# q's second addend by an accumulating DMA, pairs of exponential tiles added on VectorE, the overflow chain in pieces, three splits earlier

## The chip, the cores and the metric

The kernel runs on one core of one Trainium2 chip. Its metric is the device time in microseconds (us) of the slowest core, here the only one; the time of a kernel is the median of its runs. Besides the timed runs there is one profiled execution, from which all rows below come.

## What is computed

Three stages follow each other, each on the result of the one before. The reference, cut to what matters:

```python
q_pool = q.reshape(B, H, S // 2, 2, D).mean(axis=3)       # B 2, H 8, S 1152, D 64
scores = scale * np.matmul(q_pool, k.transpose(0, 1, 3, 2))
attn = np.exp(scores - np.max(scores, axis=-1, keepdims=True))
attn = attn / (np.sum(attn, axis=-1, keepdims=True) + 1e-09)
x = np.matmul(attn, v)                                    # then (1152, 512)

e_idx = np.argmax(x @ w_gate, axis=1)                     # 8 experts, one for each token
...
h = np.maximum(x[mask] @ w1[e], 0.0)                      # 512 to 1024
out[mask] = gate_w[mask, None] * eom[mask, e, None] * (h @ w2[e])

h = x @ w_in                                              # 512 to 2048
g = h * np.tanh(log1p(exp(h)))
return g @ w_out                                          # 2048 to 512
```

The weights of the last stage come as 64-bit floats; the kernel makes 32-bit ones of them ("decodes" them) on VectorE.

## The kernel before, in words

The order of instructions on each engine is the order in which the program writes them; nothing reorders them, and an engine that waits holds all that is behind it in its own queue. Products in full precision are made of three products of a high and a low part (mm3): the high part is a copy to a rounded 32-bit type on ScalarE (act, L91), the low part the difference, on VectorE (tt, L94, or stt, L97).

**Attention** (0 to 300 us) works on eight pairs of heads. The loop over g (from L499) makes nine steps for each pair p, one for each tile t of 128 keys. A step writes, in the order of seq ("0mmrpsmMt", L520): the scores of tile t (scores, L240) with their exponentials on ScalarE into the tile Pt, "pt", which has four buffers; two chunks of row maxima of the next pair (max_chunk, L201: a matmul into one of three PSUM tiles "mx" and a maximum on VectorE, L103); for the step before, the products of exponentials and v (pv, L262) and the row sums of the exponentials (psums, L268: eight matmuls of 160 columns by e2); and one or two more chunks of maxima. Each chunk first takes one task of the step off a list (mxc). The tasks stand in a table (at_step, L411): the loading of the next pair's k and q (load_head, L159, on SP's queue), the sum of the two addends of q's mean (qsum, L174; VectorE, for two heads of 16 GpSimd), the high and low parts of q and k (qhi, qlo, khi, klo), the reciprocals of the pair before (sum_rec), its output (x_out, x_put). At the end of the tasks of the steps in DEC_T (L171) stands one piece of decoding (decode_step, L484): three pieces make a chunk, half of one of 16 tiles wd, and the pieces are one, two and two VectorE operations. The last pair has no maxima to make for a next one; each of its steps has three pieces. DEC_A is the number of chunks that attention decodes, DEC_M the number done when the experts end.

**Routing** (300 to 318 us) takes each token's expert and place. The experts (318 to 471 us) are eight slots of fixed room, three wide ones and five narrow ones; tokens without room go to an overflow loop (L1091 on), whose passes are left out where there are none. The slots' steps form one list, flat, and the loop over q (L1052) writes for step q the preparations of step q + 2 and then its products. The first layer makes hps and its high and low parts hh and hl; the second layer uses them with the parts w2h and w2l of w2. At q = 2 stands routing_over (L701): 28 operations on VectorE that find the overflowing tokens' places, from cap to oi. At q = 4 routing_oix (L742) takes oi through nine small matmuls (L745); then the routing's pool is closed and a pool mq is opened in its room, and from there pieces of decoding follow each step of a wide slot (DECS, L1017). One chunk of 32 is left for the last stage.

**The last stage** (477 to 701 us) makes 48 steps of zmm (first layer) and omm (second layer). Ahead of it the split of wd[0..2] into high and low parts (split_hi on ScalarE, split_lo on VectorE, L1119 to L1129), then ysplit (high and low parts yh, yl of three tiles of the stage's input, from PSUM), then the first zmm (L1162), which takes the PSUM banks that the tiles of ysplit leave.

Of the kernel before, what the change touches and what calls it, by code (L numbers as in the profile page):

```python
# [9 lines left out]
F32 = mybir.dt.float32  # L10
# [74 lines left out]
def kernel(ctx, tc, cst, qt, kt, v, wgo, w1, w2, wio, out):  # L85
# [295 lines left out]
    mq = []  # L381
    wraw, dmt, dst_ = {}, {}, {}

    def load_raw(i, pool):
        f, c = divmod(i, 2)
        wraw[i] = pool.tile([P, 512, 2], I32, name="wraw", bufs=2 if pool is ap else WRB if mq and pool is mq[0] else 1)
        (A if mq and pool is mq[0] else SP).dma_start(out=wraw[i].rearrange("p a b -> p (a b)"), in_=wio[f, :, 512 * c:512 * (c + 1)].bitcast(I32))

    def decode(i, part, pool):
        f, c = divmod(i, 2)  # L390
        lo, hi = wraw[i][:, :, 0], wraw[i][:, :, 1]
        dst = wd[f][:, 512 * c:512 * (c + 1)]
        if part == 0:
            m = dmt[i] = pool.tile([P, 512], F32, name="dm", bufs=2 if pool is ap or mq and pool is mq[0] else 1)
# [24 lines left out]
    for p in range(NPAIR):  # L419
        for h, (a, b) in enumerate((((p - 2, 4), (p - 1, 0)), ((p - 1, 0), (p - 1, 3)))):  # L420
# [3 lines left out]
            at_step(lp, lt, lambda p=p, h=h: load_head(p, h))  # L424
# [18 lines left out]
    load_head(0, 0)  # L443
# [15 lines left out]
    load_head(0, 1)  # L459
# [39 lines left out]
    for g in range(-9, 9 * NPAIR):  # L499
# [4 lines left out]
        tasks = list(sched.get(g, ()))  # L504
        if p == NPAIR - 1:
# [195 lines left out]
    def routing_over():  # L701
# [29 lines left out]
        red(od, ob, ALU.add)  # L731

# [7 lines left out]
        return oi  # L740
# [81 lines left out]
    def evac(s, j):  # L822
        y = yv[0] if s > E else mq[0].tile([P, DM], F32, name="y", bufs=3)
# [186 lines left out]

    HB = 3
# [5 lines left out]
    DECS = [[0, 0, 0, 0, 0, 2, 2, 2, 2, 2], [0, 2, 2, 2, 2, 2, 2, 2, 2, 0], [0, 2, 2, 2, 2, 2, 2, 2, 2, 2]]  # L1017
# [34 lines left out]
    for q, (n_, i, _, main, w_, _) in enumerate(flat):  # L1052
# [66 lines left out]
    def split_hi(b_, f):  # L1119
        if b_ == 0:  # L1120
            hi = zp.tile([P, 1024], F32R, name="wh", bufs=NF)
            ws2[f] = [hi]
            act(hi, wd[f])

    def split_lo(b_, f, eng=V):
        if b_ == 0:
            lo = cp.tile([P, 1024], F32R, name="wd", bufs=16) if f else zp.tile([P, 1024], F32R, name="wl0")
            tt(eng, lo, wd[f], ws2[f][0].bitcast(F32), ALU.subtract)
            ws2[f].append(lo)  # L1129
# [132 lines left out]
    for i in range(len(steps) + LAG):  # L1262
        if dec[0] < 32:
            for _ in range(3 if i == 1 else 0):
                decode_step(zy, 32)
            raw_ahead(zy, 32)
# [55 lines left out]
```

## Time and profile before

| | |
|---|---|
| median of 3 runs | 708.56 us (707.39 to 708.73) |
| the profiled execution | 703.0 us, of which the span of its instructions 701.2 us |
| mean granted clock of TensorE | 0.988 of full speed |
| busy share of the span | TensorE 94%, VectorE 71%, ScalarE 53%, GpSimd 18% |
| chain of work that ended last | TensorE 21%, VectorE 7%, issue 3%, ScalarE 1% |

The busy share is an average over the three stages. PE is TensorE's matmul unit, PEld its loading of weights, DVE VectorE, ACT ScalarE, POOL GpSimd, SP the engine that mostly issues DMAs. The profiled execution lies 5.6 us below the median.

### The profile page before, as it was taken

The page shows a single profiled execution, that of the slowest core. Times are in us where ns is not written, and L with a number is a line of the kernel's source. Part 1 is how long each engine was busy: PE and PEld are TensorE (multiplying, and loading weights), DVE is VectorE, ACT ScalarE, POOL GpSimd, SP SyncE. Part 2 cuts the span into 40 slices and gives each one's busy share as a digit, 9 for nine tenths or more (in the row PEclk, how much of TensorE's full clock was granted, in tenths as well). Part 3 has the DMA queues.
Part 4 walks back from the last instruction along what each step waited for, and adds up shares of the span by engine and source line. Part 5 has one row for each costly group of instructions (what it writes and reads, how often), then busy time and mean ns, then how long its engine had stood idle before and what let it go on. Part 6 is the DMA issues. An engine that isn't in the chain of part 4 may idle for free. (4 is left out here: it accounts for less than half of the span.)

```text
span 701.2 us, 12210 instructions
## 1 busy us (share of the span) xinstructions
PE 658.6 (94%) x4719; PEld 511.8 (73%) x4719; DVE 501.1 (71%) x1022; ACT 372.2 (53%) x752; POOL 127.2 (18%) x127
## 2 busy tenths in 40 slices
PE   5999999999999999949799999986899999999997
PEld 3766666666666666628696977656787899999995
DVE  6776868686868675455764856915999977897775
ACT  6656565656475636414345536434665554555543
POOL 5200000000000000024121423211322332233322
PEclk9999999999999999989999999998999999999999
DMA  6743332433332304139579869762000020001001
GB/s 226 266 144 132 114 117 98 133 114 132 115 124 76 97 18 122 38 107 338 194 251 391 308 247 357 273 251 70 0 1 1 1 91 1 0 1 46 2 0 45
DMA packets 24915, 88.37 MB, mean 126 GB/s; under 512 B 2694, under 2 KB 7439, under 8 KB 20754
## 3 DMA queue, kind: packets, MB, share of 16 engines
q1 hardware_dynamic: 20544, 74.15, 30.1%
q10 hardware_dynamic: 2466, 8.13, 3.3%
q0 software_dynamic: 1840, 5.25, 2.2%
q8 instruction: 38, 0.62, 0.4%
q14 instruction: 27, 0.22, 0.1%
HBM read 79.65 MB, written 8.39 MB: 126 GB/s over the span
## 5 line engine op out<-in xcount | busy, mean ns | idle before, releaser
L103 DVE TENSOR_REDUCE Mp<-mx 128x1 f32<-128x384 f32 x198 | 103.6, 551 | 62.1 <-PE mx L207 61.3
L91 ACT ACTIVATE pt<-sc 128x320 f32<-128x320 f32 (+1 forms) x216 | 97.2, 489 | 89.0 <-PE sc L251 85.5
L100 POOL TENSOR_SCALAR u<-u 128x384 f32<-128x384 f32 x48 | 60.2, 1254 | 155.9 <-ACT u L91 124.1
L266 PE MATMUL pv<-pt,vt 128*64 128x288 f32 x576 | 85.8, 418 | 1.0 <-DVE sm L94 0.5
L799 PE MATMUL zps<-yh,wh 128*128 128x384 f32 x188 | 64.2, 341 | 1.7 <-DVE n L97 1.7
L207 PE MATMUL mx<-at,qs 128*128 128x384 f32 x176 | 55.8, 380 | 8.3 <-DVE qs L97 7.9
L801 PE MATMUL zps<-yl,wh 128*128 128x384 f32 x188 | 63.5, 338 | 0.0
L800 PE MATMUL zps<-yh,wd 128*128 128x384 f32 x180 | 61.0, 339 | 0.0
L1224 PE MATMUL ops<-wh,gl 128*128 128x512 f32 x144 | 57.6, 403 | 3.0 <-DVE gl L94 2.5
L266 PEld LDWEIGHTS pv<-pt,vt 128*64 128x64 f32 x576 | 35.5, 136 | 31.4 <-issue 14.5
L1224 PE MATMUL ops<-wh,gh 128*128 128x512 f32 x144 | 56.9, 395 | 0.2 <-ACT gh L91 0.2
L275 PE MATMUL pv<-pt,e 128*32 128x160 f32 x1152 | 54.0, 305 | 0.0
L275 PEld LDWEIGHTS pv<-pt,e 128*32 128x32 f32 x1152 | 30.0, 109 | 32.4 <-issue 31.5
L1224 PE MATMUL ops<-wd,gh 128*128 128x512 f32 x135 | 53.2, 394 | 0.0
L285 POOL COPY xu<-xu 128x64 f32<-128x64 f32 x8 | 1.9, 236 | 276.5 <-ACT xu L91 276.5
L207 PEld LDWEIGHTS mx<-at,qs 128*128 128x128 f32 x176 | 31.0, 195 | 23.4 <-ACT at L91 8.2
L91 ACT ACTIVATE u<-zps 128x384 f32<-128x384 f32 x48 | 23.2, 483 | 37.3 <-PE zps L801 29.9
L91 ACT ACTIVATE l<-n,two 128x384 f32<-128x384 f32 x48 | 29.5, 614 | 25.0 <-DVE n L97 25.0
L97 DVE SCALAR_TENSOR_TENSOR l<-n,r 128x384 f32<-128x384 f32 x48 | 26.6, 554 | 19.4 <-ACT r L91 19.4
L799 PEld LDWEIGHTS zps<-yh,wh 128*128 128x128 f32 x188 | 35.6, 189 | 3.6 <-ACT r L91 2.0
L1224 PEld LDWEIGHTS ops<-wh,gl 128*128 128x128 f32 x144 | 27.0, 188 | 13.9 <-DVE gl L94 7.0
L91 ACT ACTIVATE gh<-n 128x384 fp32r<-128x384 f32 x48 | 24.8, 517 | 20.7 <-DVE n L97 20.4
(272 smaller groups left out, 1584.5 us busy)
## 6 DMA issues: line engine op xcount, KB each, us to landing
wt<-in_w SPq DMA_DIRECT2D x32, 1024.0 KB, 6.9
qd<-in_qt SPq DMA_DIRECT2D x16, 576.0 KB, 3.8
kd<-in_kt SPq DMA_DIRECT2D x16, 576.0 KB, 4.9
wraw<-in_wio SPq DMA_DIRECT2D x18, 512.0 KB, 4.6
wraw<-in_wio ACTq DMA_DIRECT2D x14, 512.0 KB, 4.8
vt<-in_v SPq DMA_DIRECT2D x8, 576.0 KB, 5.2
out<-o SPq DMA_DIRECT2D x9, 256.0 KB
yt<-ybuf SPq DMA_DIRECT2D x6, 256.0 KB, 3.4
```

The costliest lines, as they stand in the source:

```text
L91: A.activation(out=out, in_=in_, func=func, **kw)
L97: V.scalar_tensor_tensor(out=out, in0=a, scalar=s, in1=b, op0=op0, op1=op1)
L100: eng.tensor_scalar(out=out, in0=a, scalar1=s1, scalar2=s2, op0=op0, op1=op1)
L103: V.tensor_reduce(out=out, in_=in_, axis=AX.X, op=op)
L207: mm(ps[:, :384], lhsT=QS[p, h][:, j * P:(j + 1) * P], rhs=At[p, h][:, cs_], start=True, stop=True)
L266: mm(pvt[p][64 * h:64 * h + 64, f, :HQ], lhsT=vt[p][:, t, h, :], rhs=Pt[p, t][:, h, f * HQ:(f + 1) * HQ], start=t == 0, stop=t == KT - 1, ...
L275: mm(pvt[p][q_:q_ + 32, f, HQ:HQ + 160], lhsT=e2[:, h], rhs=Pt[p, t][:, h, t0:t0 + 160], start=False, stop=t == KT - 1, skip_group_check=True)
L285: G.tensor_copy(xu4[:, hp, 64 * b:64 * b + 64], xu[:, o:o + 64])
L799: mm(out_, lhsT=a, rhs=c, start=first, stop=False)
L800: mm(out_, lhsT=b_, rhs=c, start=False, stop=False)
L801: mm(out_, lhsT=a, rhs=d, start=False, stop=last_)
L1224: mm(opt[b_, j], lhsT=(g_, g_, gl_)[i], rhs=(wo, wl_, wo)[i], start=f == 0 and i == 0, stop=f == NF - 1 and i == 2)
```

## The change

- **q.** load_head becomes load_q and load_k. For the first two pairs q comes as before, but into a buffer of the exponentials' tile. For pairs 2 to 7 SP loads the first addend of q's mean into tq (three buffers instead of one), and GpSimd issues a DMA that adds the second addend to it in place; the VectorE sums of these heads are gone (12 of them). The loads stand at steps 0 and 4 of pair p - 2.
- **Row sums.** add_two: at the start of steps 2, 4 and 6 VectorE adds the two exponential tiles of the two steps before into St. psums makes no sums for tiles 0, 2 and 4, and takes St in place of tiles 1, 3 and 5. A pair has six groups of eight sum matmuls instead of nine.
- **Decoding.** Its pieces stand in steps 1, 3, 5, 7 and 8 of a pair instead of 1, 2, 5, 6 and 8; attention decodes 19 chunks instead of 17, all 32 are done in attention and the experts, and the piece at the start of the last stage is gone.
- **Overflow.** routing_over is written in four pieces, at steps q = 3 to 6 of the experts, with the slot's own work between them; routing_oix follows at q = 7 instead of 4, and the pool of decoding ("dq") with it.
- **Splits.** When decoding is done, its pool is closed, and a pool wq in its room takes the high parts of wd[0..2]; their splits stand three steps of q apart, in the last slots of the experts.

```diff
-    def load_head(p, h):
-        qd[p, h] = ap.tile([P, 2, SQ], F32, name="qd", bufs=1)
-        SP.dma_start(out=qd[p, h], in_=qt[p, :, h])
+    def load_q(p, h):
+
+        if p < 2:
+            qd[p, h] = ap.tile([P, 2, SQ], F32, name="pt", bufs=4)
+            SP.dma_start(out=qd[p, h], in_=qt[p, :, h])
+        else:
+            tqt[p, h] = ap.tile([P, SQ], F32, name="tq", bufs=3)
+            SP.dma_start(out=tqt[p, h], in_=qt[p, :, h, 0])
+            G.dma_start(out=tqt[p, h], in_=qt[p, :, h, 1], accum_op=ALU.add)
+
+    def load_k(p, h):
...
-    DEC_M = 31
-    WRB = 2
-    DEC_T, DEC_A = [1, 2, 5, 6, 8], 17
+    DEC_M = 32
+    DEC_T, DEC_A = [1, 3, 5, 7, 8], 19
...
     def qsum(p, h):
-        tqt[p, h] = ap.tile([P, SQ], F32, name="tq", bufs=1)
-        tt(G if 0 < 2 * p + h < 3 else V, tqt[p, h], qd[p, h][:, 0], qd[p, h][:, 1], ALU.add)
+        if p < 2:
+            tqt[p, h] = ap.tile([P, SQ], F32, name="tq", bufs=3)
+            tt(G if 0 < 2 * p + h < 3 else V, tqt[p, h], qd[p, h][:, 0], qd[p, h][:, 1], ALU.add)
...
+    twos = (1, 3, 5)
+    St = {}
+
+    def add_two(p, t):
+        St[p] = ap.tile([P, 2, SQ], F32, name="st", bufs=1)
+        tt(V, St[p], Pt[p, t - 1], Pt[p, t], ALU.add)
+
     def psums(p, t):
 
 
+        if t + 1 in twos:
+            return
+        src = St[p] if t in twos else Pt[p, t]
         for f in range(2):
...
-                    mm(pvt[p][q_:q_ + 32, f, HQ:HQ + 160], lhsT=e2[:, h], rhs=Pt[p, t][:, h, t0:t0 + 160], start=False, stop=t == KT - 1, skip_group_check=True)
+                    mm(pvt[p][q_:q_ + 32, f, HQ:HQ + 160], lhsT=e2[:, h], rhs=src[:, h, t0:t0 + 160], start=False, stop=t == KT - 1, skip_group_check=True)
...
-            at_step(lp, lt, lambda p=p, h=h: load_head(p, h))
+            at_step(lp, lt, lambda p=p, h=h: load_k(p, h))
+            at_step(*((p - 2, 4 * h) if p > 1 else (lp, lt)), lambda p=p, h=h: load_q(p, h))
...
         tasks = list(sched.get(g, ()))
+        if p >= 0 and t - 1 in twos:
+            tasks.insert(0, lambda p=p, t=t: add_two(p, t - 1))
...
         if q == RQ:
             routing_rest()
-            oi = routing_over()
-        if q == RQ + 2:
+            over = routing_over()
+        if RQ < q <= RQ + 4:
+            oi = next(over)
+        if q == RQ + 5:
             routing_oix(oi)
...
+        if dec[0] == DEC_M and dq and not wq:
+            dstack.close()
+            wq.append(ctx.enter_context(tc.tile_pool(name="wq", bufs=1, side="right", reuse_waits="tile")))
+            q0 = q
+        elif wq and (q - q0) % 3 == 0 and len(ws2) < NPRE:
+            f = len(ws2)
+            split_hi(0, f)
+            split_lo(0, f)
...
-    for f in range(3):
-        split_hi(0, f)
-        split_lo(0, f)
     for i in range(BT):
         ysplit(i, yb[i])
```

How the instructions stand, at three places. First VectorE in attention, in steps 1 to 3 of a pair. Mp is where a maximum of the next pair goes, sm takes the sums of the pair before, Bt a low part of k, qs a low part of q, ds, dm and wd belong to decoding, st is the sum of two exponential tiles. Before:

```order
L94 TENSOR_TENSOR sm<-pv,sm 64x320
L103 TENSOR_REDUCE Mp_117<-mx 128x1
L94 TENSOR_TENSOR Bt_112<-kd,at 64x576
L103 TENSOR_REDUCE Mp_117<-mx 128x1 x2
L100 TENSOR_SCALAR ds<-wraw 128x512
L103 TENSOR_REDUCE Mp_117<-mx 128x1
L97 SCALAR_TENSOR_TENSOR qs<-tq,qs 64x576
L103 TENSOR_REDUCE Mp_117<-mx 128x1
L100 TENSOR_SCALAR dm<-dm 128x512
L97 SCALAR_TENSOR_TENSOR ds<-wraw,ds 128x512
L103 TENSOR_REDUCE Mp_117<-mx 128x1 x3
L94 TENSOR_TENSOR Bt_113<-kd,at 64x576
```

and in the changed kernel:

```order
L94 TENSOR_TENSOR sm<-pv,sm 64x320
L103 TENSOR_REDUCE Mp_117<-mx 128x1
L94 TENSOR_TENSOR Bt_112<-kd,at 64x576
L103 TENSOR_REDUCE Mp_117<-mx 128x1 x2
L100 TENSOR_SCALAR ds<-wraw 128x512
L103 TENSOR_REDUCE Mp_117<-mx 128x1
L94 TENSOR_TENSOR st<-pt 128x1152
L103 TENSOR_REDUCE Mp_117<-mx 128x1
L97 SCALAR_TENSOR_TENSOR qs<-tq,qs 64x576
L103 TENSOR_REDUCE Mp_117<-mx 128x1 x3
L94 TENSOR_TENSOR Bt_113<-kd,at 64x576
```

The add of 128x1152 stands ahead of the first maximum of step 2 and of the low part of q; the decoding piece that stood in step 2 (dm and ds) has gone to step 3.

Second VectorE in the experts, where the overflow chain ends. hl and w2l are the low parts of the hidden layer and of w2 that the slot's products wait for; ob, od, oc, oo and oi are the chain's last operations, gix<-pc what follows the small matmuls on its result. Before:

```order
L103 TENSOR_REDUCE od<-ob 128x9
L97 SCALAR_TENSOR_TENSOR od<-od,hfi 128x9
L94 TENSOR_TENSOR oc<-hfi,oc 128x9
L97 SCALAR_TENSOR_TENSOR od<-oc,od 128x9
L94 TENSOR_TENSOR oo<-od,cs 128x162
L94 TENSOR_TENSOR oi<-oo,cs 128x162
L97 SCALAR_TENSOR_TENSOR hl<-hps,hh 128x384
L94 TENSOR_TENSOR w2l<-wt,w2h 128x512
L97 SCALAR_TENSOR_TENSOR hl<-hps,hh 128x384
L94 TENSOR_TENSOR w2l<-wt,w2h 128x512
L100 TENSOR_SCALAR gix<-pc 64x9 x2
```

and in the changed kernel:

```order
L94 TENSOR_TENSOR ob<-oh,base 128x72
L103 TENSOR_REDUCE od<-ob 128x9
L97 SCALAR_TENSOR_TENSOR hl<-hps,hh 128x384
L94 TENSOR_TENSOR w2l<-wt,w2h 128x512
L97 SCALAR_TENSOR_TENSOR od<-od,hfi 128x9
L94 TENSOR_TENSOR oc<-hfi,oc 128x9
L97 SCALAR_TENSOR_TENSOR od<-oc,od 128x9
L94 TENSOR_TENSOR oo<-od,cs 128x162
L94 TENSOR_TENSOR oi<-oo,cs 128x162
L97 SCALAR_TENSOR_TENSOR hl<-hps,hh 128x384
L94 TENSOR_TENSOR w2l<-wt,w2h 128x512
L100 TENSOR_SCALAR gix<-pc 64x9 x2
```

The 28 operations of the chain, which stood in one piece from cap to oi, now stand in pieces of ten, seven, six and five, with an hl and a w2l ahead of each.

Third VectorE between the experts and the last stage. xl<-xl,gsc is the scaling of the experts' last rows, wl and wd the low parts of the split of wd[0..2], yl the low part of the last stage's input. Before:

```order
L100 TENSOR_SCALAR xl<-xl,gsc 128x512 x3
L1105 UNCONDITIONAL_BRANCH x2
L94 TENSOR_TENSOR wl_6684<-wd,wh 128x1024
L94 TENSOR_TENSOR wd<-wd,wh 128x1024 x2
L94 TENSOR_TENSOR yl<-yb_5458,yh 128x4x128
L94 TENSOR_TENSOR yl<-yb_5459,yh 128x4x128
L94 TENSOR_TENSOR yl<-yp,yh 128x4x128
L100 TENSOR_SCALAR ds<-wraw 128x512
```

and in the changed kernel:

```order
L100 TENSOR_SCALAR xl<-xl,gsc 128x512 x3
L1161 UNCONDITIONAL_BRANCH x2
L94 TENSOR_TENSOR yl<-yb_5328,yh 128x4x128
L94 TENSOR_TENSOR yl<-yb_5329,yh 128x4x128
L94 TENSOR_TENSOR yl<-yp,yh 128x4x128
L97 SCALAR_TENSOR_TENSOR n<-u 128x384
```

The three low parts of wd have left this place (they stand before the overflow loop now), and so has the decoding's ds; the first operation after yl belongs to the last stage's own chain.

## Rows read from the trace of the kernel before

**Rows 1.** The page's second part: busy tenths of the span in 40 slices of 17.5 us.
```profile
PE   5999999999999999949799999986899999999997
DVE  6776868686868675455764856915999977897775
...
PEclk9999999999999999989999999998999999999999
```

**Rows 2.** Waits of TensorE by line: us in total, times, longest.
```profile
PE zps L1162 <- DVE yl L94: 5.3, 1, 5.3
PE pc L745 <- DVE oi L94: 4.0, 1, 4.0
...
PE yb L850 <- PEq L1105: 2.3, 1, 2.3
```

**Rows 3.** Windows: us; busy us of PE, PEld, DVE, ACT, POOL; PEclk, DMA share, GB/s.
```profile
161.72:190.00 28.28, 28.19 (x269) 19.80 (x266) 22.43 (x49) 16.61 (x36) 0.24 (x1) 1.00 0.46 152
271.10:299.40 28.30, 27.61 (x292) 17.75 (x291) 14.77 (x36) 14.59 (x32) 0.24 (x1) 1.00 0.22 69
```

**Rows 4.** Timeline of TensorE in attention: start, us, engine, line, operation.
```profile
169.51 0.31 PE L249 MATMUL sc<-qs,at 128*128 128x320 f32 x1
...
186.33 0.39 PE L249 MATMUL sc<-qs,at 128*128 128x320 f32 x1
...
189.04 0.75 PE L275 MATMUL pv<-pt,e 128*32 128x160 f32 x16
189.72 0.44 PE L207 MATMUL mx<-at,qs 128*128 128x384 f32 x1
```

**Rows 5.** The tile wd: shortest, median and longest ns of one.
```profile
L94 DVE TENSOR_TENSOR wd<-wd,wh x15: 1212/1524/1528, 478.5 to 543.6; 128x1024 fp32r<-128x1024 f32 x15
```

**Rows 6.** Groups of VectorE by line: busy us, mean ns | idle before, releaser.
```profile
L97 DVE SCALAR_TENSOR_TENSOR wd<-dm,ds 128x512 int32<-128x512 int32 x32 | 24.1, 755 | 1.1
...
L94 DVE TENSOR_TENSOR tq<-qd 128x576 f32<-128x576 f32 x14 | 10.5, 748 | 4.6 <-DMA qd<-in_qt 4.6
```

**Rows 7.** Timeline of VectorE in attention, in brackets the idle time before and what ended it.
```profile
169.54 0.56 DVE L103 TENSOR_REDUCE Mp<-mx 128x1 f32<-128x384 f32 x1 [0.54 <-PE mx L207]
...
171.08 0.55 DVE L103 TENSOR_REDUCE Mp<-mx 128x1 f32<-128x384 f32 x1
```

**Rows 8.** DMA issues: queue, count, KB each, median us from issue to landing.
```profile
qd<-in_qt SPq DMA_DIRECT2D x16, 576.0 KB, 3.8
...
xg<-xbuf,gix POOLq DMA_INDIRECT x13, 7.3
```

**Rows 9.** Timeline of VectorE at the overflow chain, its first and last operations.
```profile
332.54 0.11 DVE L100 TENSOR_SCALAR cap<-pi 128x8 f32<-128x8 f32 x1
...
336.39 0.17 DVE L97 SCALAR_TENSOR_TENSOR ov<-ov,cr 128x8 f32<-128x8 f32 x1
...
340.00 0.33 DVE L94 TENSOR_TENSOR oi<-oo,cs 128x162 f16<-128x162 f32 x1
340.24 0.55 DVE L97 SCALAR_TENSOR_TENSOR hl<-hps,hh 128x384 fp32r<-128x384 f32 x1
340.71 0.68 DVE L94 TENSOR_TENSOR w2l<-wt,w2h 128x512 fp32r<-128x512 f32 x1
```

**Rows 10.** Timeline of TensorE after the overflow chain: first and tenth large matmul.
```profile
340.88 0.67 PE L799 MATMUL hps<-xh,w1h 128*128 128x384 f32 x1
...
343.90 0.36 PE L799 MATMUL hps<-xh,w1h 128*128 128x384 f32 x1
```

**Rows 11.** Windows of 2 us after the two long waits.
```profile
342.00:344.00 2.00, 2.00 (x8) 2.00 (x7) 1.18 (x6) 0.63 (x1) 0.14 (x1) 0.52 0.74 193
484.00:486.00 2.00, 2.00 (x8) 2.00 (x7) 1.19 (x3) 0.00 (x0) 0.00 (x0) 0.50 0.00 0
```

**Rows 12.** Timeline where the last stage begins, TensorE and ScalarE.
```profile
482.44 0.66 PE L1162 MATMUL zps<-yh,wh 128*128 128x384 f32 x1 [5.33 <-DVE yl L94]
...
486.66 0.49 ACT L91 ACTIVATE u<-zps 128x384 f32<-128x384 f32 x1 [7.35 <-PE zps L1166]
```

More of the change, by code (lines that the diff above doesn't have):

```diff
@@ L378, in x_put @@
         )
-    mq = []
+    dq, wq = [], []
     wraw, dmt, dst_ = {}, {}, {}
@@ L385, in load_raw @@
         f, c = divmod(i, 2)
-        wraw[i] = pool.tile([P, 512, 2], I32, name="wraw", bufs=2 if pool is ap else WRB if mq and pool is mq[0] else 1)
-        (A if mq and pool is mq[0] else SP).dma_start(out=wraw[i].rearrange("p a b -> p (a b)"), in_=wio[f, :, 512 * c:512 * (c + 1)].bitcast(I32))
+        wraw[i] = pool.tile([P, 512, 2], I32, name="wraw", bufs=2)
+        (SP if pool is ap else A).dma_start(out=wraw[i].rearrange("p a b -> p (a b)"), in_=wio[f, :, 512 * c:512 * (c + 1)].bitcast(I32))
     def decode(i, part, pool):
@@ L393, in decode @@
         if part == 0:
-            m = dmt[i] = pool.tile([P, 512], F32, name="dm", bufs=2 if pool is ap or mq and pool is mq[0] else 1)
+            m = dmt[i] = pool.tile([P, 512], F32, name="dm", bufs=2)
             s = dst_[i] = pool.tile([P, 512], I32, name="ds", bufs=1)
@@ L442 @@
     A.preload_act_table_set("natural_log_exp_and_others")
-    load_head(0, 0)
+    load_q(0, 0)
+    load_k(0, 0)
     SP.dma_start(out=cs, in_=cst)
@@ L458 @@
     qhi(0, 0)
-    load_head(0, 1)
+    load_q(0, 1)
+    load_k(0, 1)
     khi(0, 0, 0)
@@ L480, in raw_ahead @@
     def raw_ahead(pool, end):
-        while dec[2] < min(dec[0] + (2 if pool is ap else WRB if mq and pool is mq[0] else 1), end):
+        while dec[2] < min(dec[0] + 2, end):
             load_raw(dec[2], pool)
@@ L808, in evac_half @@
     def evac_half(s, y=None, r=0):
-        y = mq[0].tile([P, DM], F32, name="y", bufs=3) if y is None else y
+        y = mp_.tile([P, DM], F32, name="y", bufs=3) if y is None else y
         for d in range(2):
@@ L822, in evac @@
     def evac(s, j):
-        y = yv[0] if s > E else mq[0].tile([P, DM], F32, name="y", bufs=3)
+        y = yv[0] if s > E else mp_.tile([P, DM], F32, name="y", bufs=3)
         if s == E:
@@ L1009, in narrow_slot, with split_hi, split_lo @@
         return [(lambda i=i: pre(i), lambda i=i: main(i), lambda: None) for i in range(-1, 6)]
+    NF = FF2 // P
+    NPRE = 3
+    ws2 = {}
+    def split_hi(b_, f):
+        if b_ == 0:
+            pool, n = (wq[0], NPRE) if f < NPRE else (zp, NF - NPRE)
+            hi = pool.tile([P, 1024], F32R, name="wh", bufs=n)
+            ws2[f] = [hi]
+            act(hi, wd[f])
+    def split_lo(b_, f, eng=V):
+        if b_ == 0:
+            lo = cp.tile([P, 1024], F32R, name="wd", bufs=16) if f else wq[0].tile([P, 1024], F32R, name="wl0")
+            tt(eng, lo, wd[f], ws2[f][0].bitcast(F32), ALU.subtract)
+            ws2[f].append(lo)
     HB = 3
@@ L1078 @@
             fp.append(fstack.enter_context(tc.tile_pool(name="fps", bufs=1, space=PSUM, side="right", reuse_waits="tile")))
-            mq.append(mstack.enter_context(tc.tile_pool(name="mq", bufs=1, side="right", reuse_waits="tile")))
-            raw_ahead(mq[0], DEC_M)
-        if w_ and q > RQ + 2:
+            dstack = ExitStack()
+            dq.append(dstack.enter_context(tc.tile_pool(name="dq", bufs=1, side="right", reuse_waits="tile")))
+            raw_ahead(dq[0], DEC_M)
+        if w_ and q > RQ + 5:
             for _ in range(DECS[slots[n_][0]][i]):
-                decode_step(mq[0], DEC_M)
-            raw_ahead(mq[0], DEC_M)
-    assert dec[0] == DEC_M
+                decode_step(dq[0], DEC_M)
+            raw_ahead(dq[0], DEC_M)
+        if dec[0] == DEC_M and dq and not wq:
[6 more added lines that the diff above has]
+            split_lo(0, f)
+    assert dec[0] == DEC_M and len(ws2) == NPRE, (dec, len(ws2))
     nov = nc.values_load(ej[0:1, 8 + NOV:9 + NOV], engines=mybir.ALL_ENGINES, min_val=0, max_val=NOV)
@@ L1112 @@
     zp, zo, zy = (ctx.enter_context(tc.tile_pool(name=n_, bufs=1, side="left", reuse_waits="tile")) for n_ in ("zp", "zo", "zy"))
-    NF = FF2 // P
     NBK = TT // BT
-    ws2, yh, yl, gh, gl, opt = {}, {}, {}, {}, {}, {}
+    yh, yl, gh, gl, opt = {}, {}, {}, {}, {}
     LAG = 4
[L1119 to L1129, printed above, removed]
     yt = {}
@@ L1262 @@
     for i in range(len(steps) + LAG):
[L1263 to L1266, printed above, removed]
         for k, fn in stages.get(i, order_):
```

7 lines of the change are left out of this document (5 added, 2 removed).

## The prediction, made before the changed kernel ran

> **What bounds the kernel now.** I read the page first, then the waits of TensorE, then the timeline of three places. The slices show TensorE busy in nine tenths of nearly all forty [rows 1]; the low ones are the start, the routing between attention and the experts, the step from the experts to the last stage, and the end. So attention's time is TensorE's work, and elsewhere the gaps count. The waits of TensorE name two long ones that this change touches [rows 2]: 5.3 us for VectorE's yl ahead of the last stage, 4.0 us for VectorE's oi in the routing of the overflow. VectorE in attention is the thing to watch [rows 3]: in steps 0 to 6 of a pair of heads it is busy 22.43 of 28.28 us, while TensorE is busy 28.19.
>
> The sum is made against the profiled execution, 703.0 us with a span of 701.2. The median of the timed runs is 708.56, 5.6 us above it; I take that difference over unchanged and subtract the same gain from both.
>
> **Attention, TensorE's side.** The row sums of a step are 16 matmul records that occupy TensorE from 189.04 to 189.72, 0.68 us [rows 4]. Of nine such groups in a pair, three go: 24 groups in 8 pairs, 24 x 0.68 = 16.3 us, 2.04 a pair. That is the most it can give.
>
> **Attention, VectorE's side.** Each of the 24 adds takes two tiles of 128x1152. No add of that size is in the trace; the same operation on 1024 columns takes 1212 ns at best and 1524 at the median [rows 5], on 576 columns, for q, 748 ns [rows 6]. The first and the third give about 1.04 ns a column, so 1.34 us; with 1524 ns it would be 1.7. I take 1.36, since the slow ones stand in the last stage, where GpSimd works on SBUF beside them, and GpSimd is busy 0.24 us in this stretch [rows 3]. 24 x 1.36 = 32.6 us come, 12 sums of q at 0.75 = 9.0 us go. In steps 0 to 6 of a pair: 22.43 - 2 x 0.75 (q) - 0.9 (one decode piece of the four that lie there moves to step 7; a piece is one operation or two, the longest of them 0.755 us [rows 6], and I take 0.9 as the mean) + 3 x 1.36 = 24.1 us, of 28.28 - 2.04 = 26.24. It fits on average, 92% full, so the place decides. The add is VectorE's first task in steps 2, 4 and 6, and TensorE reaches the sums 189.04 - 186.33 = 2.71 us after a step's first matmul [rows 4]. VectorE ends the last maximum of step 1 at 171.63, 2.12 us after step 2 began at 169.51, and waited 0.54 for TensorE on the way [rows 4, 7]. With step 1 shorter by 0.68 that idle goes, and the maximum ends 2.12 + 0.68 - 0.54 = 2.26 us into the step; the add would end at 3.62, 0.9 late, or some 0.2 when step 1's decode piece is a single operation: 0.55 on average. Behind the add stand a maximum (0.55, rows 7), the low part of q, an operation as long as q's sum, and a second maximum, and TensorE's fourth maximum of that step needs the buffer that this one frees (there are three): some 0.5 more. Steps 3 to 6 have the lag's room back: two sums of q and a decode piece are gone there. I put 0.15 on them: 1.2 us a pair, a gain of 0.84, times seven pairs 5.9 us.
>
> The last pair has no maxima but the decoding: VectorE 14.77 of 28.30 us [rows 3], and now six pieces more (6 x 0.9) and three adds (4.1), 24.3 of 26.3. Its adds in steps 2, 4 and 6 stand behind the decode pieces of the step before, that in step 6 behind the reciprocals too. I expect them to give back the pair's 2.04 us: 0, between -2 and +2. **Attention: 6 us**, with 16.3 as the upper end (no wait) and -16.3 as the lower (each of 24 adds waited for in full, 24 x (1.36 - 0.68)); the value lies nearer the upper since VectorE is not full.
>
> **The q loads.** For pairs 2 to 7 SP loads one addend and GpSimd adds the other by DMA behind it, so GpSimd's queue stands still for the landing of the first. What is queued behind it is one copy of 128x64 in a pair and, in pair 0, the second half of a low part of k for pair 1; neither is wanted for several steps. A load takes 3.8 us to land, the nearest row for a DMA from GpSimd, the gather, 7.3 [rows 8]. Sum 11.1 us; the tile is wanted five steps after the issue, 5/7 x 28.28 - 3 x 0.68 = 18.2 us. Cost 0; the cover ends at 14.4 us for the second DMA. SP's queue gets the same number of loads. At the start the q tiles come from the buffers of the exponentials instead of one buffer, and the second is loaded earlier; VectorE's 27 maxima set that stretch: 0.
>
> **The overflow chain.** Now 28 VectorE operations stand in one piece, from 332.54 to 340.33, between the low parts of the hidden layer [rows 9]. TensorE waits 4.0 us for the end of it [rows 2], then runs nine matmuls from 340.88 to 343.90 at a granted clock of 0.52, the lower of the levels 1.2 and 2.4 GHz [rows 10, 11]. At the full clock nine take about half, 1.6 us: 1.4 lost. The change spreads the chain over four steps of the expert and moves the nine small matmuls on its result three steps back. The largest piece, up to the operation that starts at 336.39, is 4.0 us, the other three share the 3.8 behind it; VectorE's own work in a step, a low part of hidden and one of w2, is 0.55 and 0.68 [rows 9]. A step of TensorE is 21 matmuls, nine of which are 1.6 us: 3.7 us. So one step of VectorE runs over, by 1.5 us, and the low parts are used two steps after they are made. Gain 4.0 + 1.4, less 0.2 for small waits: **5.2 us**, between 0 (still behind each other) and 5.4. Decoding in the experts starts three steps later but has one chunk less and 39 pieces in the same three wide experts: 0.
>
> **From the experts to the last stage.** TensorE has waited 5.33 us when it starts the last stage's first matmul at 482.44 [rows 12], so add_rows ended at 477.1. In between VectorE runs three low parts of w (3 x 1.22 [rows 5]) and only then the yl, which free the PSUM banks that TensorE needs. The change has these three, and their three ScalarE halves, in the last two experts, in a slice in which VectorE is busy one tenth of the time [rows 1]: 0, or 0.3 us if one delays a relu on ScalarE. Then the yl follow ScalarE's yh at once; the last pair of them takes about as long as two of VectorE's operations of 0.6, so the first matmul starts at about 478.3. A wait of 1.2 instead of 5.3 us keeps the clock: the wait of 2.3 us a little earlier lies in a slice whose clock is in the highest tenth [rows 1, 2]. From the first matmul to the first u pass 486.66 - 482.44 = 4.2 us at 0.50 of the clock [rows 11, 12]; half of it is 2.1, and as part of it is no streaming I take 2.5. So u starts at 480.8, 5.9 us earlier, and from there VectorE's chain sets the pace as before. The decode of the last chunk also goes; it stood while TensorE made that first group, ahead of anything VectorE could do: 0. **6 us**, between 3.7 (the splits alone) and 7.
>
> **Sum.** 6 + 5.2 + 6 = 17.2 us: 708.56 - 17.2 = 691.4 us (the profiled execution 703.0 - 17.2 = 685.8).
>
> **The rivals.**
> A, the forecast: about 691.4, from 685 to 697; 0.51.
> B, TensorE hardly waits in attention: VectorE has 2 us a pair left by the average above. Then 16.3 + 5.3 + 6.5 = 28 us: 680.5. Against it is the order in step 2. 0.22.
> C, VectorE becomes attention's bound and takes the 16.3 back or a little more (-3 us, adds of 1.5 us): 708.56 + 3 - 11.2 = 700.4. 0.17.
> D, the other side: the added q comes late. ScalarE's high part of q would wait, the exponentials stand behind it in its queue, and TensorE behind those. It costs from 14.4 us for the second DMA on; at 15.9, 2.2 times the gather, each of 12 loads costs 1.45 us and the whole gain is gone; at 18 us 12 x 3.6 = 43 us are lost: 734. For it: no DMA that adds is in the trace. Against it: the DMA engines are under half busy here (0.46, rows 3). As the rows stand: 0.06. The Trainium skill (SBUF — State Buffer, "Who interferes with whom") says that a DMA from GpSimd waits for its descriptors while VectorE holds the port they share, in copies and tensor_scalar of certain forms; by that rule the decode pieces would hold an issue back. No row here shows it; by that rule alone D would be likelier, at the same price of 1.45 us a load and upward.
> E, the change doesn't do what it says in the overflow: a piece still holds back a low part, and TensorE waits in smaller portions: 691.4 + 4 = 695.4. 0.04.
>
> **How the numbers follow.** The time is that of A. The range must leave out no more than 2 in 10: from 679, just below B, to 703, just past C; it leaves out D, and the tails of B and C. What a measurement of this kernel tells from no change is about 0.2%, 1.4 us. Faster: A, B, E and most of C, 0.89. The same: 0.02 of C. Slower: D and 0.03 of C, 0.09.
>
> **What would show it.** In the profile after: 960 records of row sums instead of 1152, 24 adds of 1.3 to 1.4 us; a pair about 34.0 us long instead of 34.86 (32.8 in B, 35 or more in C); TensorE's waits in step 2 of a pair for the sum tile; no 4 us wait for oi and no half clock there; the wait ahead of the last stage down to about 1.2 us, with the clock at 1.00. The prediction is wrong if a pair's length doesn't shorten by 0.3 to 1.6 us, if ScalarE waits for a DMA of tq, or if either gap comes back elsewhere.

## The result, and the profile of the changed kernel

The changed kernel took 702.25 us (median of 4 runs, 698.68 to 704.62) against 708.64 (4 runs); the ratio is 0.9919, with a 95% interval of 0.9890 to 0.9948. With more runs of both it was 701.14 (8 runs) against 706.81 (19 runs, 704.47 to 710.62), ratio 0.9917 (0.9889 to 0.9946). So 5.7 us are gained, where 17.2 were forecast. The direction was right and the time lies in the range, near its upper end, but a third of the gain is there.

The profiled execution took 704.62 us with a span of 702.6: it is the longest of its four, and that of before (703.0) lay below all 19 runs of the larger set. Executions of one kernel differ by some 3 us either way, so the two traces, taken whole, show no gain. Their stages do. The page's busy tenths in 40 slices, to be read against [rows 1]:

```profile
PE   4999999999999999859989999968899999999997
DVE  6896969787787978556554848732999977897775
...
PEclk9999999999999999979999999998999999999999
```

VectorE is fuller in attention (slices 1 to 16). The waits of TensorE by line (us in total, times, longest), which answer to [rows 2]:

```profile
PE pv L294 <- DVE st L94: 4.9, 8, 2.0
...
PE yb L879 <- DVEq L1161: 3.2, 1, 3.2
PE hps L988 <- ACT hr L91: 2.5, 2, 1.3
...
PE yp L826 <- ACT hh L91: 2.3, 1, 2.3
PE zps L1204 <- DVE yl L94: 2.2, 1, 2.2
```

The 4.0 us for oi are gone and the 5.3 for yl have become 2.2. New are the wait for the sum tile st, which was forecast, and three that were not: for ScalarE's hh and hr in the experts, and for VectorE's branch (DVEq L1161), the join behind the overflow loop.

The table has the stages in us, each from a start in TensorE's timeline to the next: x0, x1, ... are the transposes of gathered rows (xps<-cs,xg) in their order, yb and zps the first matmuls of these names at the end of the experts, ops the first of the last stage's second layer. All columns but before and after are runs told of below.

| stage | before | before_again | after | after_again | dec_late | split_late | best |
|---|---|---|---|---|---|---|---|
| start | 24.2 | 24.4 | 24.8 | 23.5 | 23.6 | 24.6 | 24.4 |
| first pair | 32.84 | 33.08 | 31.58 | 32.82 | 34.11 | 31.80 | 31.69 |
| pairs 1 to 6 | 210.84 | 210.83 | 205.44 | 205.43 | 205.42 | 205.48 | 205.50 |
| last pair, to pc<-oh | 37.75 | 37.74 | 39.94 | 38.39 | 38.38 | 38.41 | 37.72 |
| routing, to x0 | 9.27 | 9.34 | 9.34 | 9.63 | 9.33 | 9.37 | 9.63 |
| x0 to x1 (overflow chain) | 35.87 | 36.25 | 30.63 | 30.26 | 30.45 | 30.51 | 28.84 |
| x1 to x2 | 17.31 | 17.31 | 22.30 | 20.97 | 17.96 | 19.81 | 17.96 |
| x2 to x5 | 52.97 | 52.94 | 54.72 | 53.72 | 52.96 | 53.79 | 53.07 |
| x5 to x6 | 23.45 | 23.39 | 23.35 | 24.32 | 26.39 | 23.44 | 25.57 |
| x6 to yb | 26.49 | 27.21 | 29.02 | 30.74 | 28.74 | 29.17 | 27.75 |
| yb to zps | 11.49 | 11.49 | 13.31 | 13.41 | 14.07 | 8.38 | 10.25 |
| zps to ops | 14.71 | 14.91 | 14.10 | 12.53 | 12.57 | 14.06 | 14.05 |
| ops to the last matmul | 199.58 | 199.57 | 199.59 | 199.54 | 199.57 | 199.60 | 199.53 |

Attention and the overflow chain gained nearly what was forecast. The experts behind x1 lost 9.0 us (mean of the two traces of either kernel, 120.5 to 129.6), where 0 was forecast: 4.3 of it in x1 to x2, 3.0 in x6 to yb. And yb to ops gained nothing (26.3 to 26.7), where 6 was forecast. The traced runs of the two kernels differ by 1.2 us (means 704.4 and 703.2) where the medians differ by 5.7, so the 9.0 may be too large by up to 4.5; the places are the same in both traces of the changed kernel.

**Attention, step 2.** TensorE's and VectorE's timeline in pair 4, counted from 0 (start, us, in brackets the idle time before):

```profile
165.31 0.32 PE L257 MATMUL sc<-qs,at 128*128 128x320 f32 x1
...
168.78 0.75 PE L294 MATMUL pv<-st,e 128*32 128x160 f32 x16 [0.76 <-DVE st L94]
...
170.63 0.44 PE L215 MATMUL mx<-at,qs 128*128 128x384 f32 x1 [0.20 <-DVE Mp L103]
170.91 0.31 PE L257 MATMUL sc<-qs,at 128*128 128x320 f32 x1
```

```profile
166.91 0.55 DVE L103 TENSOR_REDUCE Mp<-mx 128x1 f32<-128x384 f32 x1
167.38 1.35 DVE L94 TENSOR_TENSOR st<-pt 128x1152 f32<-128x1152 f32 x1
168.65 0.55 DVE L103 TENSOR_REDUCE Mp<-mx 128x1 f32<-128x384 f32 x1
169.23 0.76 DVE L97 SCALAR_TENSOR_TENSOR qs<-tq,qs 64x576 fp32r<-64x576 f32 x1
```

The last maximum of step 1 ends 2.15 us into step 2 (forecast 2.26), the add ends 3.42 in, TensorE waits 0.76 for it and 0.20 for a maximum. Over pairs 1 to 6 step 1 is shorter by 0.68 us, step 3 by 0.72 and step 5 by 0.59; step 2 is longer by 0.95 and step 4 by 0.12. The tile st (ns: shortest, median, longest) shows the add at the estimate of 1.36:

```profile
L94 DVE TENSOR_TENSOR st<-pt x24: 1337/1349/1352, 32.6 to 283.7; 128x1152 f32<-128x1152 f32 x24
```

**Behind the overflow chain.** ScalarE's timeline at q = 8, the step after decoding's loads are first issued, then TensorE's, then windows (us; busy us of PE, PEld, DVE, ACT, POOL; PEclk, DMA share, GB/s):

```profile
348.00 0.97 ACTq L406 DMA_DIRECT2D wraw<-in_wio  x2
355.30 0.69 ACT L91 ACTIVATE dm<-wraw 128x512 f32<-128x512 f32 x1 [7.91 <-DMA wraw<-in_wio]
355.89 1.15 ACT L91 ACTIVATE w2h<-wt 128x512 fp32r<-128x512 f32 x2
...
359.96 0.60 ACT L91 ACTIVATE hh<-hps 128x512 fp32r<-128x512 f32 x1
```

```profile
360.62 0.50 PE L826 MATMUL yp<-w2h,hh 128*128 128x512 f32 x1 [2.25 <-ACT hh L91]
...
362.60 0.63 PE L826 MATMUL yp<-w2h,hh 128*128 128x512 f32 x1
```

```profile
348.00:355.00 7.00, 7.00 (x51) 6.43 (x50) 0.00 (x0) 0.00 (x0) 0.00 (x0) 1.00 0.76 275
362.00:364.00 2.00, 2.00 (x5) 1.07 (x4) 0.69 (x1) 0.94 (x2) 0.99 (x1) 0.50 0.91 332
```

The first load of decoding takes 7.2 us; the first pieces of decoding wait for it and stand ahead of the next expert's parts on ScalarE and VectorE, so both engines do nothing for 7 us. Then TensorE waits 2.25 us and runs at the lower of its two clock levels, 0.63 us a matmul. In the kernel before, VectorE began the first piece 5.5 us after the issue (timeline of ScalarE and VectorE, then the window of the load):

```profile
342.13 0.98 ACTq L387 DMA_DIRECT2D wraw<-in_wio  x2
...
347.60 0.43 DVE L100 TENSOR_SCALAR ds<-wraw 128x512 int32<-128x512 int32 x1 [1.21 <-DMA wraw<-in_wio]
```

```profile
342.13:347.60 5.47, 5.47 (x25) 5.07 (x24) 2.26 (x9) 1.64 (x3) 1.29 (x1) 0.83 0.93 321
```

More was moved beside the load there than in the changed kernel (321 GB/s, against 275 in 348 to 355), so what made it longer is open. What its length costs is not: in the seven traces of this order that show the landing, it came after 5.72 to 7.22 us, and TensorE's wait for hh was that time less 4.95 us in each (0.78 in split_late, 1.46 in split_zp, 2.25 in after).

In x6 to yb the last load of decoding does the same. ScalarE, then TensorE, in the changed kernel:

```profile
451.50 0.69 ACT L91 ACTIVATE dm<-wraw 128x512 f32<-128x512 f32 x1 [4.08 <-DMA wraw<-in_wio]
```

```profile
453.49 0.44 PE L988 MATMUL hps<-cs,hr 128*128 128x128 f32 x2 [1.22 <-ACT hr L91]
```

hr stands behind dm in ScalarE's queue. In the kernel before, ScalarE stood 1.97 us there and TensorE waited for no hr. Another 1.6 us TensorE waits there for hn, which stands behind ScalarE's issue of xl (the next rows); in before_again it was 1.1.

**The early splits.** VectorE's, ScalarE's and TensorE's timeline from the last narrow expert on:

```profile
461.10 1.23 DVE L94 TENSOR_TENSOR wd<-wd,wh 128x1024 fp32r<-128x1024 f32 x1 [2.30 <-ACT wh L91]
467.82 1.23 DVE L94 TENSOR_TENSOR wd<-wd,wh 128x1024 fp32r<-128x1024 f32 x1 [5.50 <-ACT wh L91]
...
470.39 1.46 DVE L100 TENSOR_SCALAR xl<-xl,gsc 128x512 f32<-128x512 f32 x3
```

```profile
462.44 1.93 ACTq L869 DMA_DIRECT2D xl<-ybuf  x3
464.48 0.38 ACT L91 ACTIVATE hn<-hps 128x256 f32<-128x256 f32 x1 [2.95 <-DMA ybuf<-y,six]
...
466.75 1.05 ACT L91 ACTIVATE wh<-wd 128x1024 fp32r<-128x1024 f32 x1
```

```profile
471.10 0.38 PE L877 MATMUL yb<-tri,zero 128*128 128x512 f16 x1 [1.99 <-PEq L1161]
474.63 2.08 PE L879 MATMUL yb<-cs,xl 128*128 128x128 f32 x8 [3.15 <-DVEq L1161]
...
484.41 0.48 PE L1204 MATMUL zps<-yh,wh 128*128 128x384 f32 x1 [2.23 <-DVE yl L94]
```

The third high part stands behind a DMA that ScalarE issues only after a scatter; VectorE waits 5.50 us for it with the scaling of the last rows (xl) in its queue, comes to the join late, and TensorE waits 3.15 us there.

### The profile page after: what moved, and what is told of

It is laid out like the page before. It is cut to its first block, busy times and chain, and to the rows that moved or that the text cites. A ratio compares the mean times of both kernels' runs of the same rounds, so it can differ in the third digit from the quotient of the medians.

```text
span 702.6 us, 11490 instructions
## 1 busy us (share of the span) xinstructions
PE 649.7 (92%) x4335; PEld 503.0 (72%) x4335; DVE 521.1 (74%) x1034; ACT 369.8 (53%) x752; POOL 138.3 (20%) x139
## 5 line engine op out<-in xcount | busy, mean ns | idle before, releaser
L215 PE MATMUL mx<-at,qs 128*128 128x384 f32 x176 | 57.3, 383 | 10.4 <-DVE qs L97 8.4
L91 ACT ACTIVATE gh<-n 128x384 fp32r<-128x384 f32 x48 | 24.8, 517 | 20.6 <-DVE n L97 20.4
L828 PEld LDWEIGHTS zps<-yl,wh 128*128 128x128 f32 x188 | 35.3, 188 | 0.0
L100 DVE TENSOR_SCALAR dm<-dm 128x512 f32<-128x512 f32 x64 | 29.7, 464 | 7.4 <-ACT dm L91 7.3
L91 ACT ACTIVATE dm<-wraw 128x512 f32<-128x512 f32 x32 | 21.7, 678 | 25.0 <-DMA wraw<-in_wio 17.0
```

The lines of the kernel that those rows point to most:

```text
L91: A.activation(out=out, in_=in_, func=func, **kw)
L100: eng.tensor_scalar(out=out, in0=a, scalar1=s1, scalar2=s2, op0=op0, op1=op1)
L215: mm(ps[:, :384], lhsT=QS[p, h][:, j * P:(j + 1) * P], rhs=At[p, h][:, cs_], start=True, stop=True)
L828: mm(out_, lhsT=a, rhs=d, start=False, stop=last_)
```

## The experiments

Theory 1: the gains are there, and are given back behind decoding's first loads and behind the third early split. Its rivals stand with each run.

**after_again**: the changed kernel, unedited.

> The changed kernel once more, with more rounds. Theory 1 (the gains of attention and of the overflow chain are there, and are given back by waits behind the first loads of decoding and behind the third early split): 702 us, 6 us below the kernel before, and in the trace again a wait of about 2 us for the high part of hidden at the first narrow expert (hh) and of about 3 us for VectorE at the join after the overflow loop. Theory 2 (the losses of the one trace are chance, since its four runs lie 6 us apart): these two waits are gone or elsewhere in another run, and the median is below 700.

701.14 us. TensorE waited 2.0 us for hh and 2.0 for VectorE at the join, in the same places. It is no chance, though the size of the first moves with the load's landing (6.93 us here).

**no_two**: which part of attention's gain is the adds'.

```diff
-    twos = (1, 3, 5)
+    twos = ()
```

> The changed kernel with all nine groups of row sums in a pair again and no adds of exponential tiles; the q loads stay. Theory 1: the seven pairs lose the 0.95 us each that they gained, the last pair loses less: 5 to 7 us above the changed kernel, 707 to 709. Rival (the adds take back what the sums give, and the gain in attention came from VectorE's freed sums of q): within 1.5 us of the changed kernel.

705.58 us, ratio 0.9977 (0.9952 to 1.0001) to before, 4.4 above the changed kernel, where theory 1 had 5 to 7. A pair of the middle takes 34.9 us, as before the change: pairs 1 to 6 lose 5.0 us (210.47 together), and the last pair gains 0.65 (37.74). The adds make attention's gain; VectorE's freed sums of q make at most 0.4 us of it (210.84 before the change).

**twos246**: the adds one step later.

```diff
-    DEC_T, DEC_A = [1, 3, 5, 7, 8], 19
+    DEC_T, DEC_A = [1, 2, 4, 6, 8], 19
...
-    twos = (1, 3, 5)
+    twos = (2, 4, 6)
```

> The changed kernel with the pairs of tiles (1,2), (3,4), (5,6), so that the adds stand first in steps 3, 5 and 7, and the pieces of decoding in steps 1, 2, 4, 6 and 8. Theory 1 (what a pair loses, 0.95 of 2.04 us, is lost in step 2, because a maximum, a piece of decoding and the low part of q stand round the add there): step 2 falls to 3.6 to 4.3 us, a pair of the middle from 34.2 to 33.2 to 33.7. Rival (any place loses as much, VectorE is too full): another step grows by as much, a pair 34.0 or more.

One run: 712.78 us. The groups of sums (0.68 us) go from steps 2, 4 and 6 here, and from 1, 3 and 5 in the changed kernel, so each is held against the kernel before (means of pairs 1 to 6). Step 2 takes 4.03 us instead of 4.35, 0.36 more than without its group; the changed kernel loses 0.95 there. But step 5, which has the reciprocals, rises from 4.53 to 5.20 and step 7 from 2.99 to 3.77. A pair takes 35.14 us, as before the change, and the last pair 41.47. The rival holds: step 2 is the change's own worst place, but steps 5 and 7 together are worse ones.

**q_step1**: the first pair differs by up to 2.8 us between traces with the new q loads.

```diff
-            at_step(*((p - 2, 4 * h) if p > 1 else (lp, lt)), lambda p=p, h=h: load_q(p, h))
+            at_step(*((p - 2, 4 * h or 1) if p > 1 else (lp, lt)), lambda p=p, h=h: load_q(p, h))
```

> The changed kernel with the first q load of a pair one step later, so that in the first pair GpSimd makes the second half of its low part of k before its queue stands still for the landing of the first addend. Theory 1 (GpSimd's late low part runs beside VectorE's sum of q, which then takes 1.3 to 2.4 us instead of 0.76 and holds back a maximum that TensorE needs): the sum takes 0.76 us, step 1 of the first pair 3.9 us at most (3.86 to 6.26 in five of six traces of the changed q loads, 2 where the start was late), the first pair 31.6 us. Rival (it is the DMA's traffic at the start): the sum still takes 1.3 us or more.

One run: 701.91 us. The first pair takes 31.70 us, its step 1 3.39. VectorE's sum of q there, first in dec_late, with GpSimd's low part of k beside it, then in q_step1, without:

```profile
26.46 2.38 DVE L94 TENSOR_TENSOR tq<-pt 128x576 f32<-128x576 f32 x1
```

```profile
27.46 0.76 DVE L94 TENSOR_TENSOR tq<-pt 128x576 f32<-128x576 f32 x1
```

Theory 1 holds, by these rows: the first pair was as short in after (31.58), where the sum took 1.32 us and step 1 3.95. In after_again the two were 2.22 and 4.84, in dec_late 2.38 and 6.25. The Trainium skill (SBUF — State Buffer, "Who interferes with whom") has the rule: a VectorE operation with two inputs in SBUF contends with a GpSimd one that reads SBUF. These rows agree, 2.38 us beside it and 0.76 alone.

**dec_late**: decoding kept out of the first wide expert.

```diff
-    DECS = [[0, 0, 0, 0, 0, 0, 0, 0, 2, 2], [0, 2, 2, 2, 2, 2, 2, 2, 2, 2], [0, 2, 2, 2, 2, 2, 2, 2, 2, 1]]
+    DECS = [[0, 0, 0, 0, 0, 0, 0, 0, 0, 0], [2, 2, 2, 2, 2, 2, 2, 2, 2, 2], [2, 2, 2, 2, 2, 2, 2, 2, 2, 1]]
```

> The changed kernel with the four pieces of decoding of the first wide expert put into the second one, so that the first piece comes ten steps or more after its load. Theory 1: TensorE no longer waits 2.25 us for hh nor runs at half clock behind it, 4 to 5 us below the changed kernel, about 697.5. Theory 2 (chance, or the load of weights itself): no change, 702, and a wait of the same size in the same place.

700.06 us, 0.9895 (0.9872 to 0.9918). The place is mended: the wait is gone and x1 to x2 takes 17.96 us. The same window in its trace, to be held against the one above:

```profile
348.00:355.00 7.00, 7.00 (x52) 6.51 (x51) 2.58 (x4) 4.35 (x8) 3.53 (x4) 1.00 0.91 333
```

The load is still there (5.9 us; 7.3 in both_late, with x1 to x2 the same), but nothing stands behind it. The time moved by 1.1 instead of 4 to 5, less than the spread of the runs; x1 to yb is 3.5 us shorter (126.1), and the four pieces cost 2 to 3 us where they went (x5 to x6).

**before_again**: the kernel before, unedited.

> The kernel before once more, for a second trace: its one trace (703.0 us) lies below all its timed runs (704.47 to 710.62). Theory 1: attention (243.7 us from the first pair's first scores to the last pair's) repeats within 0.5 us, and the difference lies in the experts, where loads of weights and of decoding share the DMA engines. Rival: it is spread evenly, as a slower clock would spread it.

705.71 us, one run. Its pairs and last stage repeat within 0.25 us; of its 1.8 us, 1.1 are in x0 to x1 and x6 to yb. That is where theory 1 has them, but no trace caught a long run of before, so the rest of its spread stays unexplained.

**split_late**: the splits back ahead of the last stage, in decoding's room.

```diff
-        elif wq and (q - q0) % 3 == 0 and len(ws2) < NPRE:
-            f = len(ws2)
-            split_hi(0, f)
-            split_lo(0, f)
...
+    for f in range(3):
+        split_hi(0, f)
+        split_lo(0, f)
     for i in range(BT):
         ysplit(i, yb[i])
```

> The changed kernel with the three splits put back ahead of the last stage. Theory 1: VectorE's scaling of the last rows is no longer held behind the third high part, the 3.15 us wait at the join goes, but the three low parts (3.7 us) stand ahead of the last stage again: 0 to 3 us below the changed kernel, 699 to 702. Rival (the early splits are worth their 3.7 us and more): 4 to 6 us above it, 706 to 708.

699.35 us, 0.9891 (0.9863 to 0.9919): undoing the early splits costs nothing. And yb to zps took 8.38 us, not the 11 or more that three low parts ahead of yl should take. So the low parts had not been what the wait before was made of.

**split_zp**: as split_late, in the pool zp that the splits had before the change.

```diff
-            pool, n = (wq[0], NPRE) if f < NPRE else (zp, NF - NPRE)
+            pool, n = zp, NF
...
-            lo = cp.tile([P, 1024], F32R, name="wd", bufs=16) if f else wq[0].tile([P, 1024], F32R, name="wl0")
+            lo = cp.tile([P, 1024], F32R, name="wd", bufs=16) if f else zp.tile([P, 1024], F32R, name="wl0")
```

> The changed kernel with the three splits back ahead of the last stage and in the pool that they had before the change, instead of in the room that decoding left. Theory 1 (the 5.3 us wait before was not for three low parts in a row, but for the room: the first low part waited 8.4 us until TensorE had read the tile whose room it takes): the low part waits for the end of TensorE's yp again, and from yb to the first zps it is 11.5 us, 3 us longer than with the splits late but in the free room (8.4): 702 to 703. Rival (the room makes no difference): 8.4 us, 699.4.

703.74 us (703.34 without the longest of twelve runs), 0.9954 (0.9924 to 0.9984), and 11.97 us from yb to zps. The first low part in the kernel before, in split_zp and in split_late:

```profile
477.21 1.23 DVE L94 TENSOR_TENSOR wl<-wd,wh 128x1024 fp32r<-128x1024 f32 x1 [8.38 <-PE yp L882]
```

```profile
475.34 1.23 DVE L94 TENSOR_TENSOR wl<-wd,wh 128x1024 fp32r<-128x1024 f32 x1 [8.35 <-PE yp L909]
```

```profile
468.24 1.22 DVE L94 TENSOR_TENSOR wl<-wd,wh 128x1024 fp32r<-128x1024 f32 x1 [5.08 <-ACT wh L91]
```

In zp the low part waits until TensorE has ended yp; in decoding's room it starts behind ScalarE's high part, beside TensorE's yb. The room is what this part of the change gains, some 3 us.

**split_near**: the early splits, one step apart.

```diff
-        elif wq and (q - q0) % 3 == 0 and len(ws2) < NPRE:
+        elif wq and q - q0 >= 3 and len(ws2) < NPRE:
```

> The changed kernel with the three early splits at steps 50, 51 and 52 of the experts instead of 50, 53 and 56, so that the third high part stands ahead of ScalarE's loads of the last rows (which wait for a scatter) and not behind them. Theory 1 (it is the third split that is late: VectorE waits 5 to 7 us for it, with the scaling of the last rows behind): no wait of VectorE at the join, 8.4 us from yb to the first zps instead of 13.3, and 2 to 4 us below the changed kernel, 697 to 699. Rival (any split there delays ScalarE's small high parts in the last narrow experts by as much as it saves): the 8.4 us, but 2 us and more in the narrow experts on top, 700 to 702.

698.30 us, 0.9866 (0.9836 to 0.9896), 2.8 below the changed kernel. The wait at the join is 0.26 us, so it was the third split. The 8.4 us were missed: yb to zps took 11.8, with the clock at 0.61 in 467.70 to 476.00.

**both_late**: dec_late and split_late together.

> The changed kernel with decoding kept out of the first wide expert and the splits back ahead of the last stage (in decoding's room). Theory 1: the two losses are in different places, and their repair adds up but for what the denser decoding costs in the later wide experts (3 us in the run with decoding late): 696 to 699. Rival: one repair only moves the wait, 699 to 700 as each alone.

696.09 us, 0.9876 (0.9835 to 0.9917): x1 to x2 17.96, yb to zps 8.38, x5 to x6 26.56. Together 5.0 us below the changed kernel, where they gave 1.1 and 1.8 alone: one repair does not only move the wait, and the rival falls.

**both_late_last**: and no adds in the last pair.

```diff
-        if p >= 0 and t - 1 in twos:
+        if 0 <= p < NPAIR - 1 and t - 1 in twos:
...
-        if t + 1 in twos:
+        if t + 1 in twos and p < NPAIR - 1:
             return
-        src = St[p] if t in twos else Pt[p, t]
+        src = St[p] if t in twos and p < NPAIR - 1 else Pt[p, t]
```

> As the one before, and the last pair makes its nine groups of row sums without adds. Theory 1: the last pair takes 32.2 instead of 32.9 us, 0.6 us less: 695.5 to 698.5, not to be told from the one before by the time, but by the pair's length in the trace. Rival (the adds gain in the last pair too): the pair takes 33 us or more.

697.13 us, 0.9871 (0.9831 to 0.9912), by the time the same. The stage of the last pair is 37.74 us instead of 38.40: its adds lose 0.66.

**best**: both_late_last with q_step1, and 20 chunks decoded in attention.

```diff
-    DEC_T, DEC_A = [1, 3, 5, 7, 8], 19
+    DEC_T, DEC_A = [1, 3, 5, 7, 8], 20
...
+    DECS = [[0, 0, 0, 0, 0, 0, 0, 0, 0, 0], [0, 2, 2, 2, 2, 2, 2, 2, 2, 2], [0, 2, 2, 2, 2, 2, 2, 2, 2, 2]]
```

> All repairs together: q loads at steps 1 and 4, 20 chunks decoded in attention (room for it in the last pair, which makes no adds), so that the first wide expert has no piece and the two others have 18 each beginning with their second step, and the splits ahead of the last stage in decoding's room. Theory 1: attention as in the changed kernel less 0.6 in the last pair; 18 us from the second to the third gather's transposes; 23.5 us where the denser decoding took 26.5; 8.4 us from yb to the first zps: 693 to 696, 11 to 14 us below the kernel before. Rival (the waits go where they can, behind the loads of weights): 696 to 699.

692.37 us (5 runs, 691.57 to 694.04) against 706.55, ratio 0.9801 (0.9776 to 0.9827): 14.2 us below the kernel before and 9 below the changed one, and the five runs lie within 2.5 us. The time is a little below the 693 to 696 expected, though two stages missed theirs. x5 to x6 took 25.57 instead of 23.5: TensorE waited there in several pieces for hl, w1l and w2h. yb to zps took 10.25 instead of 8.4, with the clock at 0.72 in its first six us.

## Why the prediction was wrong

- **TensorE's side of attention and the price of an add**: right in its price, 0.68 us a group, and an add took 1.349 us (1.36 forecast). The count of records that I gave as a sign was wrong: 768 of the 1152 are left, not 960, since each of the 24 groups has 16.
- **Step 2 and the pairs**: right, by the steps given. Step 2 cost 0.95 (0.55 + 0.5 forecast), steps 3 to 6 cost 0.17 (0.15), a pair of the middle gained 0.90 (0.84). The two parts of step 2 missed in opposite directions: in pair 4 TensorE waited 0.76 us for the add and 0.20 behind it, so that their sum fits so well is in part luck. Rival B fell with that, and C too: VectorE was busy 27.83 of the 34.14 us of pair 4, so it was the place that decided.
- **The last pair**: 0 forecast, 0.65 lost in after_again and 2.2 in the first trace, just past the 2 given as its range.
- **"At the start ...: 0"**: wrong in its reason. GpSimd's queue stood still for the first addend, as forecast, and the low part behind it was not wanted soon; but run late it contended with VectorE's sum of q. The first pair ranged from 31.6 to 34.4 us.
- **The q loads**: right. The second DMA landed in 4.0 to 5.7 us (eleven of after_again's twelve show it; 14.4 was the cover), and no engine on the path waited for it. Rival D fell. GpSimd's issues of it took 0.85 to 1.13 us, so the rule of the Trainium skill named there (SBUF — State Buffer, "Who interferes with whom") had no price for them in this run.
- **The overflow chain**: 5.2 forecast, 5.6 found (36.1 to 30.4, means of two traces), of which some 0.5 has only moved behind x1, where the nine small matmuls on oi now stand. No wait for oi, no lower clock.
- **"Decoding in the experts starts three steps later ...: 0"**: this step failed. The lead of the load over its first piece, one step, did not change, but three steps later the next expert's parts stand behind that piece, and the load came after 7.2 us instead of 5.5. x1 to x2 lost 4.3 us; with the pieces elsewhere it is 17.96, 0.65 above before, whether the load takes 5.9 us (dec_late) or 7.3 (both_late). The 0 was the price of moving a queue, which I had not followed past the pieces to what stands behind them. The wait for hr behind decoding's last load, 1.2 of the 3.0 us lost in x6 to yb, is of the same kind.
- **"From the experts to the last stage", 6 us**: this step failed in two places. I read the 5.33 us of [rows 12] as three low parts in VectorE's queue. The wait of the first of them, 8.38 us for TensorE's yp, stood in the same timeline, unread: they were late for their room. And I costed the early place by VectorE's busy share [rows 1], without following the third high part in ScalarE's queue, where a DMA's wait held it. The room is worth some 3 us, the early order cost more than that; together 0 (yb to ops 26.3 before, 22.4 with the room alone in split_late, 26.7 with both). Two smaller terms were off too. The wait for yl is 2.2 us, not 1.2, in every trace with the new room. And the clock was not kept each time: in the 3 us from the first zps it was 0.53 in the first trace, as slow as before (0.50), and 1.00 in after_again (zps to ops 14.10 and 12.53).
- **The sum.** 17.2 forecast; 5.7 by the runs. That 702 lies near rival C's 700.4 is no merit of C: attention gained what A said, and the loss stands where no rival looked.

What stays open: even best needs 3 to 4 us more than before from x1 to yb (124.4 against 120.2 and 120.9). Its engines wait there in small pieces, the longest TensorE's 3.4 us at the join (2.3 before); no run tells them apart. Why decoding's first load lands after 5.7 us in one run and 7.3 in another is open too.

## What to carry to other kernels

When a wait names the last of several instructions in a queue, read what the first of them waited for: the queue's length explains the wait only if its head was ready. When work moves to an idle engine, follow the slowest of its inputs through that other engine's queue, DMA issues included, and ask what is queued behind the one that waits; a busy share of a tenth is no cover. A load that landed 7.2 to 7.3 us after its issue cost TensorE 2.25 us of wait where other work stood behind its first user (after), and none where nothing did (both_late).

## What the runs showed of the hardware

The same operation on VectorE took 0.76 us alone and up to 2.82 us (both_late) beside GpSimd's subtraction. After waits of nearly the same length (2.4 to 2.5 us for the branch) TensorE's granted clock stayed at 1.00 in split_late (466 to 472 us), was 0.61 in split_near (467.7 to 476.0) and 0.72 in both_late_last (467.6 to 473.6), windows with the columns as above:

```profile
466.00:472.00 6.00, 5.62 (x48) 5.55 (x49) 3.19 (x3) 2.95 (x3) 0.12 (x2) 1.00 0.52 161
```

```profile
467.70:476.00 8.30, 8.00 (x41) 7.22 (x42) 0.00 (x0) 0.00 (x0) 0.10 (x1) 0.61 0.39 118
```

```profile
467.60:473.60 6.00, 6.00 (x37) 5.78 (x38) 3.67 (x3) 2.95 (x3) 0.10 (x1) 0.72 0.50 165
```

In split_late VectorE and ScalarE worked on the splits meanwhile, in split_near they stood still; but in both_late_last they worked as much as in split_late. What made the difference the traces do not show. The first load of decoding (512 KB, on ScalarE's queue) landed after 5.7 to 7.3 us in the ten traces that show it; the most traffic did not go with the longest landing (7.2 us at 275 GB/s in after, 5.9 at 333 in dec_late).
